# Attention and a routed expert layer on one core: side columns copied once per chunk, the last batch's routing moved by one slot, the first z chunk loaded in halves

## The chip, the cores and the metric

The kernel runs on one core of a Trainium2 chip. The metric is the device time of one execution in microseconds; the number that is compared is the median of several runs. One further execution is recorded by the hardware profiler, and all rows below come from that one.

## The reference

Eight batches of 2496 tokens, 256 wide. The first part is an attention without a softmax, gated by `u`; its result is the input of a layer of eight experts, of which each token uses one.

```python
scores = (1 / S) * z @ z.T            # per batch, z is 2496 x 64
x = u * (relu(scores) ** 2 @ v)       # 19968 rows of 256
logits = x @ w_gate + bias[modality]  # 8 experts
e = argmax(logits); gate = softmax(logits)[e]
out[row] = gate * (relu(x[row] @ w1[e]) @ w2[e])   # w1: 256 x 1024, w2: 1024 x 256
```

Everything is float32. The kernel gets the accuracy out of faster matmuls by splitting each operand into a high part and a low rest (`zm`, `vh`/`vl`, `ah`/`al`, `xh`/`xl`, `hh`/`hl`), and by multiplying high with high, high with low and low with high.

## The kernel before

**Phase 1** walks over the batches, in each over 5 chunks of up to 512 query columns, and in each chunk over ten steps of two blocks of 128 keys. A step is: scores on TensorE (L294), relu on ScalarE (L300), the square (L314), its split into `ah` (L338, ScalarE or VectorE) and `al` (L347, VectorE), and the product with `v` on TensorE (L363). At a chunk's end the sum is read out, transposed back to rows (L448) and multiplied by `u` (`take_rows`), so that `x` holds 4 blocks of 128 tokens ("columns", 20 in a batch). Each column then gets its eight logits on VectorE (L470, eight instructions of 256 elements), later the routing (`route_logits` to `route_gates`), which yields for each token a place in the list of its expert, and a scatter: VectorE copies the token's gate and number, two values, behind the 256 of its row (L581), and GpSimd writes the column's 128 rows to their places in DRAM with an indirect DMA (L583).

**Phase 2** walks over tiles of 512 rows of one expert (`run_tile`). A tile has slots f = 0 to 7 and two more. In slot f TensorE multiplies with a block of `w1` (`up`, L1048, the first matmul with `xh`, the second with `xl`), ScalarE takes the relu (`hh`, L1052), VectorE makes the rest (`hl`, L1053), and two slots later TensorE multiplies with `w2` (`down`, L1061 with `hh`, L1062 with `hl`). `finish` casts the row numbers (`ids`, L1072), scales the result on ScalarE and VectorE (L1077, L1079: four instructions `y`), and GpSimd scatters it to the output. The next tile's rows are transposed on VectorE (`xt`, L890) in slot 6 (slot 4 in the tile before tile -2), copied on ScalarE (`xh`, L897), and subtracted on VectorE (`xl`, L902).

Four tiles, t = -4 to -1, run before all tokens are routed. Into their 32 slots (slot 0 is tile -4, f = 0; slot 8 is tile -3, f = 0) a table of `put(slot, piece)` calls places what is left of the last batch: logits, four pieces of routing, the scatters of its last twelve columns, the plan of the remaining tiles (eight pieces, one-partition arithmetic on VectorE, L626 to L716), and the loads of the first planned weights. The engines run their instructions in the order in which the program issues them (`manual_schedule`), so the table sets the order on VectorE by hand. An instruction that comes late on VectorE makes every later `hl`, `xl` and `y` late.

At the **program's start** the SyncE queue issues the loads of `z` and `v` (L226, L157) in turn; TensorE runs matmuls on zeros (`warm`, L923) until `zm` is there: ScalarE makes its high part (L231), VectorE its low part (L236).

Of the kernel before, what the change touches and what calls it, by code (L numbers as in the profile page):

```python
# [9 lines left out]
F32 = mybir.dt.float32  # L10
# [3 lines left out]
ALU = mybir.AluOpType  # L14
AX = mybir.AxisListType
P = 128
T = 512
# [4 lines left out]
def ins_of(x):  # L22
    return getattr(x, "ins", x)
# [3 lines left out]
def tile_attention_moe(ctx: ExitStack, tc: tile.TileContext, u, v, zt, mid, wg, mb, w1, w2, out):  # L27
# [11 lines left out]
    nc = tc.nc  # L39
    B, S, D = u.shape  # L40
# [5 lines left out]
    J = T // P  # L46
# [5 lines left out]
    XW = D + 2  # L52
# [37 lines left out]
    def bank_tile(shape, name):  # L90
        return bank["pool"].tile(shape, F32, tag=bank["tag"], name=name)
# [4 lines left out]
    few = 128  # L96
# [27 lines left out]
    n = NCOL - J  # L124
# [97 lines left out]
    Z, V, zraw, vraw, U = {}, {}, {}, {}, {}  # L222

    def load_z(b, c):
        zr = raw.tile([P, T], F32, tag="zr", bufs=3, name="zr")
        nc.sync.dma_start(out=zr, in_=zt[b, :, c * T:(c + 1) * T])  # L226
        zraw[b, c] = zr

    def prep_z_high(b, c):
        zm = turned.tile([P, 2, T], F32R, tag="zm", bufs=NCH + 1, name="zm")  # L230
        nc.scalar.copy(out=zm[:, 0, :], in_=zraw[b, c])  # L231
        Z[b, c] = zm

    def prep_z_low(b, c):
        zm = Z[b, c]
        nc.vector.tensor_tensor(out=zm[:, 1, :], in0=zraw.pop((b, c)), in1=zm[:, 0, :].bitcast(F32), op=ALU.subtract)  # L236

    def load_v(b, c):
        vr = raw.tile([P, J, D], F32, tag="vr", bufs=3, name="vr")
# [223 lines left out]
    def logits(b, c, n):  # L463

        if c == 0 and n == 0:
            LG[b] = rows.tile([P, NCOL, E], F32, tag="lg", bufs=2, name="lg")
        x = X[b, c]
        for k in range(n * LG_STEP, (n + 1) * LG_STEP):
            j, e = k // E, k % E
            nc.vector.scalar_tensor_tensor(  # L470
                out=spare[:, k % 2, :],
                in0=x[:, j, 0:D],
                scalar=1.0,
                in1=wgb[:, e, :],
                op0=ALU.mult,
                op1=ALU.mult,
                accum_out=LG[b][:, c * J + j, e:e + 1],
            )
# [4 lines left out]
    RT = {}  # L483
# [92 lines left out]
    def scatter(b, k):  # L576

        c, j = k // J, k % J
        x = X[b, c]
        n = 64 if k == NCOL - 1 else P  # L580
        nc.vector.tensor_copy(out=x[:, j, D:XW], in_=RT[b]["side"][:, k, :])  # L581
        i = ins_of(
            nc.gpsimd.indirect_dma_start(  # L583
                out=xs,
                out_offset=bass.IndirectOffsetOnAxis(ap=RT[b]["sloti"][:n, k:k + 1], axis=0),
                in_=x[:n, j, :],
                in_offset=None,
                bounds_check=E * CAP - 1,
                oob_is_err=False,
            )  # L590
        )
        tc.declare_no_dep(i, group="xs", reason="each token has a row of its own")
        tc.add_to_no_dep_group("xs", i)
        scatters.append(i)
        if j == J - 1:
            X.pop((b, c))
# [149 lines left out]
    for b in range(B):  # L746
        g0 = b * per
        if b:
            for c in range(NCH):
                gz = g0 - 13 + 2 * c if c else g0 - 24  # L750
                gv = g0 - NI + 2 * c if c else g0 - 20
                at(gz - 3, load_z, b, c)
                at(gv - 3, load_v, b, c)
                queue(gz, g0 + 2 * c - 8, act(0.6, prep_z_high, b, c), dve(0.7, prep_z_low, b, c))
                queue(gv, g0 + 2 * c - 2, act(1.05, prep_v_high, b, c), dve(1.25, prep_v_low, b, c))
        for c in range(NCH):
            g = g0 + c * NI
            at(g + 5, load_u, b, c)
            at(g + NI - 1, evacuate_low, b, c, 0)
            at(g + NI - 1, evacuate_low, b, c, 1)  # L760
            if b < B - 1 or c < NCH - 1:
                for h in reversed(range(KD)):
                    queue(g + NI, g, dve(0.7, evacuate_high, b, c, h))
                at(g + NI, make_rows, b, c)
                for r in range(2):
                    queue(g + NI + 1, g + NI + 2, dve(0.7, take_rows, b, c, r))
                for n in range(LGN):
                    hurry = b == B - 2 and c == NCH - 1 or b == B - 1 and c == 1
                    queue(g + NI + 2, g + NI + ((7 if b < B - 1 else 5) + n // 3 if hurry else 8 + n // 2), dve(0.35 * LG_STEP, logits, b, c, n))

    def routing(b):

        pause = none(lambda: None)
        cols = WHOLE if b < B - 1 else SOON
        pieces = [dve(2.0, route_logits, b, cols), dve(1.9, route_places, b, cols), pause, none(route_count, b, cols)]
        pieces += [dve(2.6, lambda b: (route_slots(b, cols), route_gates(b, cols)), b)]
        hurry = J if b < B - 1 else 0
        pieces += [dve(0.2, lambda k=k: (scatter(b, k), scatter(b, k + 1))) for k in range(0, hurry, 2)]
        for k in range(hurry, cols.stop):
            pieces += [dve(0.1, scatter, b, k)] + [pause] * (b != B - 2)  # L780
        return pieces

    for e in range(E):
        for n in range(2):
            k = 2 * e + n
# [11 lines left out]
    for c in range(2, NCH):  # L797
        queue(max(1, 2 * c - 4), max(1, 2 * c - 4), act(0.6, prep_z_high, 0, c), dve(0.7, prep_z_low, 0, c))
        queue(2 * c - 2, 2 * c - 2, act(1.05, prep_v_high, 0, c), dve(1.25, prep_v_low, 0, c))
# [116 lines left out]
    for c in range(3):  # L916
        load_z(0, c)
        load_v(0, c)
    with tc.manual_schedule(engines={ET.PE, ET.Activation, ET.DVE, ET.Pool}):
        warm = [bank_tile([P, T], "warm") for _ in halves]  # L920
        for n in 4 * [few] + 6 * [T]:
            for x, h in zip(warm, halves):
                nc.tensor.matmul(out=x[:, 0:n], lhsT=zeros[h, 0:P], rhs=zeros[h, 0:n], start=True, stop=True)  # L923
        prep_z_high(0, 0)
        prep_z_low(0, 0)
        prep_v_first()
        scores(0)
# [4 lines left out]
        prep_z_low(0, 1)  # L932
        scores(1, True)
        load_z(0, 3)
        load_v(0, 3)
        square(1)
# [30 lines left out]
        for g in range(G):  # L967
            waiting += [(end, g, p) for end, p in due.pop(g, ())]
            b, c, i = steps[g]
# [217 lines left out]
    def put(slot, *pieces):  # L1187
        n, f = slots[slot]
        between[n][f] += pieces
# [1 line left out]
    put(0, lambda: part_weights_low(-1, KD))  # L1191
    put(3, lambda: part_weights_low(-1, KD + 1))
    for n, args in enumerate(left_over):
        put((1, 1, 11)[min(n, 2)], lambda args=args: logits(*args))
    for slot, n in zip((2, 3, 4, 4, 4, 5, 5, 5, 6, 7, 9, 9, 9, 10, 10, 10), range(LGN)):
        put(slot, lambda n=n: logits(B - 1, NCH - 1, n))
    for slot, pieces in ((12, (route_logits, route_exp)), (13, (route_places,)), (15, (route_count,)), (16, (route_slots, route_gates))):
        put(slot, *(lambda p=p: p(B - 1, LATE) for p in pieces))
    for n, k in enumerate(range(LATE.start, NCOL)):
        put(16 + n * 3 // 4, lambda k=k: scatter(B - 1, k))  # L1200
    planning = plan()
    for slot in (17, 18, 19, 20, 20, 21, 21, 22):
        put(slot, lambda: next(planning, None))
    put(22, lambda: fetch_weights(0))
    put(27, lambda: prefetch(-1), lambda: fetch_weights(1))
# [70 lines left out]
```

## Time and profile before

| | us |
|---|---|
| median of 3 runs | 2238.99 (2238.19 to 2239.13) |
| the profiled execution | 2237.93 |
| its span | 2236.1 |
| TensorE busy | 2213.1 (99%) |
| VectorE busy | 1805.5 (81%) |
| ScalarE busy | 1574.0 (70%) |
| GpSimd busy | 364.4 (16%) |
| mean granted clock | 0.996 of full speed |

The span is the time between the first and the last instruction of the profile; the profiled execution's own time is 1.83 us longer. The engines work side by side, so a busy share alone says little of a change in one place. The queries below look at the waits of TensorE and at the places that the table of slots touches. In the rows PE is TensorE, PEld its weight loads, DVE VectorE, ACT ScalarE, POOL GpSimd; `out<-in` names the buffers; a bracket at the end of a timeline row is the engine's idle time just before and what ended it.

### The profile page before, as it was taken

Reading aid. Unit: us, or ns where it says so; the run is one execution under the profiler, and the core shown is the slowest. Engines: PE = TensorE matmul, PEld = TensorE weight load, DVE = VectorE, ACT = ScalarE, POOL = GpSimd, SP = SyncE. Lnnn points to the kernel's source line nnn. Section 1 sums busy time; section 2 is a strip of 40 time slices with the busy share of each in tenths; the row PEclk is TensorE's granted clock in tenths of the full one; section 3 lists DMA queues with packets and bytes.
Section 4 is the critical chain, followed back from the end, with each engine's and each line's share of the span. In section 5 each row is a group of like instructions: output and inputs, shape, how many; then the busy total and the mean of one; then the engine's idle time right before and its main releaser. Section 6 shows DMA issues by size and latency. Waiting matters only on the chain.

```text
span 2236.1 us, 44437 instructions
## 1 busy us (share of the span) xinstructions
PE 2213.1 (99%) x16850; PEld 1867.1 (83%) x16850; DVE 1805.5 (81%) x4555; ACT 1574.0 (70%) x1919; POOL 364.4 (16%) x350
## 2 busy tenths in 40 slices
PE   9999999999999999999999999999999999999996
PEld 7888888888888888888888888788888888888885
DVE  7889989989989989989989998666666666666664
ACT  8888888888888888888888873455555555555553
POOL 0000220220220220220220422221212121111111
PEclk9999999999999999999999999999999999999998
DMA  6223223222112112112111122654545454545440
GB/s 195 102 71 106 78 92 113 74 77 76 34 58 75 34 57 75 36 58 73 39 47 39 51 89 62 180 167 119 164 122 162 123 161 124 159 124 160 127 150 23
DMA packets 199602, 216.64 MB, mean 97 GB/s; under 512 B 118448, under 2 KB 166064, under 8 KB 194512
## 3 DMA queue, kind: packets, MB, share of 16 engines
q1 hardware_dynamic: 184288, 172.49, 26.3%
q0 software_dynamic: 15088, 41.21, 5.0%
q8 instruction: 134, 2.20, 0.4%
q14 instruction: 92, 0.75, 0.1%
HBM read 168.23 MB, written 62.19 MB: 103 GB/s over the span
## 4 chain that ended last, share of the span: by engine, by line
PE 59%; issue 26%; DMA 9%; POOL 3%; DVE 1%; ACT 0%; POOLq 0%
PE acc L363 46%; PE s L294 12%; DMA out_dram<-y,ids 9%; POOL out_dram L1081 3%; PE po L448 1%; POOL xs L583 0%; POOLq L1081 0%; PE warm L923 0%; DVE hl L1053 0%; ACT r L298 0%; ACT vh L245 0%; ACT r L300 0%; ACT r L314 0%; ACT zm L231 0%; PE pc L547 0%
## 5 line engine op out<-in xcount | busy, mean ns | idle before, releaser
L300 ACT ACTIVATE r<-s 128x1024 f32<-128x1024 f32 (+1 forms) x395 | 397.4, 1006 | 180.9 <-PE s L294 176.2
L347 DVE TENSOR_TENSOR al<-r,ah 128x1024 fp32r<-128x1024 f32 (+1 forms) x359 | 429.6, 1197 | 78.1 <-ACT ah L338 61.6
L470 DVE SCALAR_TENSOR_TENSOR spare<-x,wgb 128x256 f32<-128x256 f32 x1280 | 462.2, 419 | 0.9
L1052 ACT ACTIVATE hh<-ph 128x512 fp32r<-128x512 f32 x312 | 186.3, 597 | 384.1 <-PE ph L1048 384.1
L1061 PE MATMUL po<-w,hh 128*128 128x512 f32 x1248 | 447.4, 394 | 0.0
L363 PE MATMUL acc<-ah,vh 64*128 64x512 f32 (+1 forms) x3120 | 434.4, 382 | 0.8 <-DVE ah L321 0.8
L1048 PE MATMUL ph<-xh,w 128*128 128x512 f32 x1248 | 427.4, 393 | 0.3 <-DVE x L418 0.3
L363 PE MATMUL acc<-al,vh 64*128 64x512 f32 (+1 forms) x3120 | 426.5, 381 | 0.0
L363 PE MATMUL acc<-ah,vl 64*128 64x512 f32 (+1 forms) x3120 | 424.8, 382 | 0.0
L314 ACT ACTIVATE r<-r 128x1024 f32<-128x1024 f32 (+2 forms) x401 | 416.9, 1040 | 3.3
L1053 DVE SCALAR_TENSOR_TENSOR hl<-ph,hh 128x512 fp32r<-128x512 f32 x312 | 215.4, 690 | 213.9 <-ACT hh L1052 213.6
L583 POOL DMA_INDIRECT xs<-x,sloti x160 | 204.5, 1278 | 1000.0 <-DVE x L581 953.8
L1062 PE MATMUL po<-w,hl 128*128 128x256 f32 x1248 | 349.4, 280 | 2.6 <-DVE hl L1053 2.6
L363 PEld LDWEIGHTS acc<-ah,vh 64*128 64x128 f32 x3120 | 299.6, 184 | 55.2 <-DVE ah L321 1.3
L363 PEld LDWEIGHTS acc<-al,vh 64*128 64x128 f32 x3120 | 299.8, 184 | 54.8
L363 PEld LDWEIGHTS acc<-ah,vl 64*128 64x128 f32 x3120 | 292.5, 184 | 54.5
L294 PE MATMUL s<-zm 64*128 64x512 f32 (+1 forms) x2400 | 336.8, 386 | 0.7 <-ACT r L300 0.7
L338 ACT CAST ah<-r 128x1024 fp32r<-128x1024 f32 (+1 forms) x282 | 287.1, 1018 | 0.0
L1061 PEld LDWEIGHTS po<-w,hh 128*128 128x128 f32 x1248 | 235.0, 188 | 54.3
L1048 PEld LDWEIGHTS ph<-xh,w 128*128 128x128 f32 x1248 | 234.8, 188 | 54.4 <-DVE x L418 0.7
L1081 POOL DMA_INDIRECT out_dram<-y,ids x157 | 152.8, 973 | 706.8 <-DVE y L1079 678.7
L294 PEld LDWEIGHTS s<-zm 64*128 64x128 f32 x2400 | 221.8, 185 | 40.2 <-ACT r L300 1.4
(164 smaller groups left out, 1955.7 us busy)
## 6 DMA issues: line engine op xcount, KB each, us to landing
w<-w1s SPq DMA_DIRECT2D x37, 1024.0 KB
w<-w2s SPq DMA_DIRECT2D x37, 1024.0 KB
xg<-xs SPq DMA_DIRECT2D x156, 128.0 KB
vr<-in_v_dram SPq DMA_DIRECT2D x32, 512.0 KB
ut<-in_u_dram SPq DMA_DIRECT2D x32, 512.0 KB
zr<-in_zt_dram SPq DMA_DIRECT2D x40, 256.0 KB
w1s<-in_moe_w_dram SPq DMA_DIRECT2D x16, 512.0 KB
w2s<-in_moe_w_dram SPq DMA_DIRECT2D x8, 1024.0 KB
```

What stands on the lines that cost most here:

```text
L294: nc.tensor.matmul(out=s[t][:, :w], lhsT=lhs, rhs=mv[halves[t], ql, :w], start=n == 0, stop=n == 2)
L300: nc.scalar.activation(out=r[:, :, :w], in_=both[:, :, :w], func=AF.Relu, scale=INV)
L314: nc.scalar.square(out=a[:, t, :w], in_=r[:, t, :w])
L338: copy(out=ah[:, :, :w], in_=st_a[g][:, :, :w])
L347: nc.vector.tensor_tensor(out=al[:, :, :w], in0=a[:, :, :w], in1=ah[:, :, :w].bitcast(F32), op=ALU.subtract)
L363: nc.tensor.matmul(out=acc[b, c][r][dh][:, :w], lhsT=V[b, k // J][y][halves[r], k % J, dh * P:(dh + 1) * P], rhs=x[halves[r], k % 2, :w], ...
L470: nc.vector.scalar_tensor_tensor(out=spare[:, k % 2, :], in0=x[:, j, 0:D], scalar=1.0, in1=wgb[:, e, :], op0=ALU.mult, op1=ALU.mult, accum ...
L1048: nc.tensor.matmul(out=ph, lhsT=lhs, rhs=rhs[:, k, :], start=n == 0, stop=n == 3 * KD - 1)
L1053: nc.vector.scalar_tensor_tensor(out=hl, in0=ph, scalar=0.0, in1=hh.bitcast(F32), op0=ALU.max, op1=ALU.subtract)
L1061: nc.tensor.matmul(out=po[j], lhsT=hh[:, s], rhs=both, start=f == 0, stop=False, skip_group_check=True)
L1062: nc.tensor.matmul(out=po[j][:, 0:D], lhsT=hl[:, s], rhs=w[:, 0, :], start=False, stop=f == KF - 1, skip_group_check=True)
L1081: nc.gpsimd.indirect_dma_start(out=out, out_offset=bass.IndirectOffsetOnAxis(ap=ids[:, j:j + 1], axis=0), in_=y, in_offset=None, bounds_ch ...
```

## The change

Three edits. The copy of gate and token number is issued once per chunk, for its four columns together, before the chunk's first scatter, and no longer in front of each scatter. In the table of slots the last batch's routing, scatters and plan come one slot earlier, and the last two of the four left-over units of logits of the chunk before come in slot 7 and no longer in slot 11. The first chunk of `z` is loaded, copied and subtracted in two halves of 256 columns, and one pair of the `warm` matmuls is left out.

```diff
--- before.py
+++ after.py
@@ -223,17 +223,24 @@
 
     def load_z(b, c):
         zr = raw.tile([P, T], F32, tag="zr", bufs=3, name="zr")
-        nc.sync.dma_start(out=zr, in_=zt[b, :, c * T:(c + 1) * T])
+
+        n = 1 if b or c else 2
+        for i in range(n):
+            s = slice(i * T // n, (i + 1) * T // n)
+            nc.sync.dma_start(out=zr[:, s], in_=zt[b, :, c * T + s.start:c * T + s.stop])
         zraw[b, c] = zr
 
     def prep_z_high(b, c):
         zm = turned.tile([P, 2, T], F32R, tag="zm", bufs=NCH + 1, name="zm")
-        nc.scalar.copy(out=zm[:, 0, :], in_=zraw[b, c])
+        for s in (slice(0, T),) if b or c else (slice(0, T // 2), slice(T // 2, T)):
+            nc.scalar.copy(out=zm[:, 0, s], in_=zraw[b, c][:, s])
         Z[b, c] = zm
 
     def prep_z_low(b, c):
         zm = Z[b, c]
-        nc.vector.tensor_tensor(out=zm[:, 1, :], in0=zraw.pop((b, c)), in1=zm[:, 0, :].bitcast(F32), op=ALU.subtract)
+        zr = zraw.pop((b, c))
+        for s in (slice(0, T),) if b or c else (slice(0, T // 2), slice(T // 2, T)):
+            nc.vector.tensor_tensor(out=zm[:, 1, s], in0=zr[:, s], in1=zm[:, 0, s].bitcast(F32), op=ALU.subtract)
 
     def load_v(b, c):
         vr = raw.tile([P, J, D], F32, tag="vr", bufs=3, name="vr")
@@ -578,7 +585,8 @@
         c, j = k // J, k % J
         x = X[b, c]
         n = 64 if k == NCOL - 1 else P
-        nc.vector.tensor_copy(out=x[:, j, D:XW], in_=RT[b]["side"][:, k, :])
+        if not j:
+            nc.vector.tensor_copy(out=x[:, :, D:XW], in_=RT[b]["side"][:, k:k + J, :])
         i = ins_of(
             nc.gpsimd.indirect_dma_start(
                 out=xs,
@@ -918,7 +926,7 @@
         load_v(0, c)
     with tc.manual_schedule(engines={ET.PE, ET.Activation, ET.DVE, ET.Pool}):
         warm = [bank_tile([P, T], "warm") for _ in halves]
-        for n in 4 * [few] + 6 * [T]:
+        for n in 4 * [few] + 5 * [T]:
             for x, h in zip(warm, halves):
                 nc.tensor.matmul(out=x[:, 0:n], lhsT=zeros[h, 0:P], rhs=zeros[h, 0:n], start=True, stop=True)
         prep_z_high(0, 0)
@@ -1191,15 +1199,15 @@
     put(0, lambda: part_weights_low(-1, KD))
     put(3, lambda: part_weights_low(-1, KD + 1))
     for n, args in enumerate(left_over):
-        put((1, 1, 11)[min(n, 2)], lambda args=args: logits(*args))
+        put((1, 1, 7)[min(n, 2)], lambda args=args: logits(*args))
     for slot, n in zip((2, 3, 4, 4, 4, 5, 5, 5, 6, 7, 9, 9, 9, 10, 10, 10), range(LGN)):
         put(slot, lambda n=n: logits(B - 1, NCH - 1, n))
-    for slot, pieces in ((12, (route_logits, route_exp)), (13, (route_places,)), (15, (route_count,)), (16, (route_slots, route_gates))):
+    for slot, pieces in ((11, (route_logits, route_exp)), (12, (route_places,)), (14, (route_count,)), (15, (route_slots, route_gates))):
         put(slot, *(lambda p=p: p(B - 1, LATE) for p in pieces))
     for n, k in enumerate(range(LATE.start, NCOL)):
-        put(16 + n * 3 // 4, lambda k=k: scatter(B - 1, k))
+        put(15 + n * 3 // 4, lambda k=k: scatter(B - 1, k))
     planning = plan()
-    for slot in (17, 18, 19, 20, 20, 21, 21, 22):
+    for slot in (16, 17, 18, 19, 19, 20, 21, 21):
         put(slot, lambda: next(planning, None))
     put(22, lambda: fetch_weights(0))
     put(27, lambda: prefetch(-1), lambda: fetch_weights(1))
```

In the changed file the lines from L231 on stand 7 or 8 lines further down: L581 is L589, L890 is L898, L1053 is L1061.

The order on VectorE at the end of tile -4 (slot 7), before and then after. The rows L470 (L477 after) are the logits, two of the logits instructions and then six.

```order
L890 STREAM_TRANSPOSE xt<-xg 128x1024
L1053 SCALAR_TENSOR_TENSOR hl<-ph,hh 128x512
L470 SCALAR_TENSOR_TENSOR spare,lg<-x,wgb 128x256 x2
L902 TENSOR_TENSOR xl<-xt,xh 128x1024
L1072 CAST ids<-gate 128x4
L1079 SCALAR_TENSOR_TENSOR y<-po,gate,part_19439 128x256
```

```order
L898 STREAM_TRANSPOSE xt<-xg 128x1024
L1061 SCALAR_TENSOR_TENSOR hl<-ph,hh 128x512
L477 SCALAR_TENSOR_TENSOR spare,lg<-x,wgb 128x256 x6
L910 TENSOR_TENSOR xl<-xt,xh 128x1024
L1080 CAST ids<-gate 128x4
L1087 SCALAR_TENSOR_TENSOR y<-po,gate,part_19333 128x256
```

Four more logits instructions stand between the tile's last `hl` and the next tile's `xl`.

VectorE at the end of tile -3 and the start of tile -2 (slots 15 and 16), before and after. `at` to `side` are `route_slots` and `route_gates`; `y` is the output of tile -3; `hl` is the first of tile -2.

```order
L1072 CAST ids<-gate 128x4
L1079 SCALAR_TENSOR_TENSOR y<-po,gate,part_19690 128x256
L1079 SCALAR_TENSOR_TENSOR y<-po,gate,part_19701 128x256
L1079 SCALAR_TENSOR_TENSOR y<-po,gate,part_19712 128x256
L1079 SCALAR_TENSOR_TENSOR y<-po,gate,part_19723 128x256
L1053 SCALAR_TENSOR_TENSOR hl<-ph,hh 128x512
L553 TENSOR_TENSOR at<-pc,base 128x8
L555 TENSOR_TENSOR base<-pc,base 128x8
L556 TENSOR_TENSOR run<-run,at 128x160
L557 TENSOR_TENSOR run<-run,hot 128x160
L559 TENSOR_REDUCE slot<-run 128x20
L561 CAST sloti<-slot 128x20
```

```order
L568 CAST sloti<-slot 128x20
L574 TENSOR_REDUCE sm<-ex 128x12
L575 TENSOR_SCALAR sm<-sm 128x12
L578 RECIPROCAL side<-sm 128x12
L579 TENSOR_SCALAR side<-tok 128x12
L589 COPY x<-side 128x4x2
L1080 CAST ids<-gate 128x4
L1087 SCALAR_TENSOR_TENSOR y<-po,gate,part_19602 128x256
L1087 SCALAR_TENSOR_TENSOR y<-po,gate,part_19613 128x256
L1087 SCALAR_TENSOR_TENSOR y<-po,gate,part_19624 128x256
L1087 SCALAR_TENSOR_TENSOR y<-po,gate,part_19635 128x256
L1061 SCALAR_TENSOR_TENSOR hl<-ph,hh 128x512
```

Routing stood behind tile -2's first `hl`; now it ends ahead of tile -3's `ids` and `y`, followed by one copy for the whole chunk (`128x4x2`).

VectorE at the end of tile -2 (slots 21 to 23), before and after. `p_i`, `meta` and `p_off` belong to the last two pieces of the plan.

```order
L1053 SCALAR_TENSOR_TENSOR hl<-ph,hh 128x512
L581 COPY x<-side 128x2 x2
L712 SCALAR_TENSOR_TENSOR p_i<-p_i,p_off 1x42
L713 TENSOR_TENSOR p_i<-p_i,p_last 1x42
L714 SCALAR_TENSOR_TENSOR p_i<-p_ex,p_i 1x42
L716 CAST meta<-p_i 1x42
L716 CAST meta<-p_ex 1x42
L890 STREAM_TRANSPOSE xt<-xg 128x1024
L1053 SCALAR_TENSOR_TENSOR hl<-ph,hh 128x512
```

```order
L718 TENSOR_REDUCE p_off<-p_ge 1x42
L720 SCALAR_TENSOR_TENSOR p_i<-p_i,p_off 1x42
L721 TENSOR_TENSOR p_i<-p_i,p_last 1x42
L722 SCALAR_TENSOR_TENSOR p_i<-p_ex,p_i 1x42
L724 CAST meta<-p_i 1x42
L724 CAST meta<-p_ex 1x42
L1061 SCALAR_TENSOR_TENSOR hl<-ph,hh 128x512
L898 STREAM_TRANSPOSE xt<-xg 128x1024
L1061 SCALAR_TENSOR_TENSOR hl<-ph,hh 128x512
```

The two copies behind the tile's seventh `hl` are gone, and the plan's end stands ahead of that `hl`, so that between the tile's last two `hl` only the transpose `xt` is left.

## Rows read from the trace of the kernel before

**Rows 1.** which engine is busy; section 1 of the page: busy us, share, instructions.

```profile
PE 2213.1 (99%) x16850; PEld 1867.1 (83%) x16850; DVE 1805.5 (81%) x4555; ACT 1574.0 (70%) x1919; POOL 364.4 (16%) x350
```

**Rows 2.** TensorE's waits over the run: us in total, times, longest.

```profile
PE po L1062 <- DVE hl L1053: 2.6, 2, 2.1
...
PE s L294 <- ACT r L300: 0.7, 1, 0.7
```

**Rows 3.** windows: length, busy (count) by engine, PEclk, DMA share, GB/s.

```profile
700.00:1300.00 600.00, 600.00 (x5588) 504.70 (x5586) 549.81 (x1715) 511.28 (x563) 106.83 (x86) 1.00 0.16 51
...
1407.85:1411.26 3.41, 3.41 (x13) 2.92 (x12) 2.55 (x5) 1.35 (x3) 1.92 (x3) 0.50 0.89 305
```

**Rows 4.** timeline of TensorE, end of tile -2: start, us, tile, [idle before].

```profile
1403.74 0.40 PE L1061 MATMUL po<-w,hh 128*128 128x512 f32 x1
1404.61 0.39 PE L1062 MATMUL po<-w,hl 128*128 128x256 f32 x1 [0.48 <-DVE hl L1053]
1404.84 0.39 PE L1061 MATMUL po<-w,hh 128*128 128x512 f32 x1
1407.35 0.39 PE L1062 MATMUL po<-w,hl 128*128 128x256 f32 x1 [2.12 <-DVE hl L1053]
...
1411.18 0.44 PE L1048 MATMUL ph<-xh,w 128*128 128x512 f32 x1
```

**Rows 5.** timeline of TensorE, end of tile -4 and the next tile's start.

```profile
1359.01 0.39 PE L1061 MATMUL po<-w,hh 128*128 128x512 f32 x1
...
1361.80 0.39 PE L1048 MATMUL ph<-xh,w 128*128 128x512 f32 x1
1362.03 0.40 PE L1048 MATMUL ph<-xl,w 128*128 128x512 f32 x1
```

**Rows 6.** timeline of VectorE through tile -2.

```profile
1386.50 0.69 DVE L1053 SCALAR_TENSOR_TENSOR hl<-ph,hh 128x512 fp32r<-128x512 f32 x1 [1.03 <-ACT hh L1052]
1387.11 0.15 DVE L553 TENSOR_TENSOR at<-pc,base 128x8 f32<-128x8 f32 x1
...
1389.43 0.24 DVE L581 COPY x<-side 128x2 f32<-128x2 f32 x2
...
1403.47 0.49 DVE L710 TENSOR_REDUCE p_off<-p_ge 1x42 f32<-1x336 f32 x1
1403.89 0.67 DVE L1053 SCALAR_TENSOR_TENSOR hl<-ph,hh 128x512 fp32r<-128x512 f32 x1
...
1406.64 0.65 DVE L1053 SCALAR_TENSOR_TENSOR hl<-ph,hh 128x512 fp32r<-128x512 f32 x1
```

**Rows 7.** timeline of VectorE at the end of tile -4.

```profile
1359.05 0.41 DVE L470 SCALAR_TENSOR_TENSOR spare<-x,wgb 128x256 f32<-128x256 f32 x1
...
1359.74 1.22 DVE L902 TENSOR_TENSOR xl<-xt,xh 128x1024 fp32r<-128x1024 f32 x1
```

**Rows 8.** VectorE by line, 1378.0 to 1386.6: busy us, mean ns | idle before.

```profile
L1079 DVE SCALAR_TENSOR_TENSOR y<-po,gate,part 128x256 f32<-128x256 f32 x4 | 1.9, 484 | 2.0 <-ACT part L1077 2.0
```

**Rows 9.** timeline of ScalarE at the start of the program.

```profile
3.71 0.62 ACT L231 CAST zm<-zr 128x512 fp32r<-128x512 f32 x1 [1.67 <-DMA zr<-in_zt_dram]
4.97 0.62 ACT L256 CAST vh<-vr 128x512 fp32r<-128x512 f32 x1 [0.65 <-DMA vr<-in_v_dram]
5.89 1.08 ACT L298 ACTIVATE r<-s 128x512 f32<-128x512 f32 x2 [0.29 <-PE s L294]
```

**Rows 10.** VectorE by line, 100 to 1300.

```profile
L581 DVE COPY x<-side 128x2 f32<-128x2 f32 x140 | 21.4, 162 | 0.0
```

**Rows 11.** timeline of VectorE and GpSimd: subtracts without and beside scatters.

```profile
1044.62 1.23 DVE L347 TENSOR_TENSOR al<-r,ah 128x1024 fp32r<-128x1024 f32 x1 [0.57 <-ACT ah L338]
...
1073.34 1.23 POOL L583 DMA_INDIRECT xs<-x,sloti  x1 [61.80 <-DVE x L581]
...
1075.90 1.22 DVE L347 TENSOR_TENSOR al<-r,ah 128x1024 fp32r<-128x1024 f32 x1
...
1076.22 1.76 POOL L583 DMA_INDIRECT xs<-x,sloti  x1 [0.30 <-issue]
```

## Prediction

> **What bounds the kernel now.** I read the busy shares first: TensorE is busy 99% of the span [rows 1], so a change gains only where TensorE waits or runs at a lower clock, and loses only where it makes TensorE wait. Its waits come next. They add up to little: the largest by far is the matmul with `hl` in the early tiles, 2.6 us in two pieces, and there is one of 0.7 us early in phase 1 [rows 2]. The windows show the rest of the run as TensorE's: in 600 us of phase 1 it has no idle time, beside a VectorE busy 549.81 us; but for 3.41 us after 1407.85 its granted clock is 0.50, which of the two levels is 1.2 GHz and not 2.4 [rows 3]. The timeline puts the two waits and that stretch at one place, the end of tile -2 (slots 22 and 23): idle 0.48 us, 2.12 us, and then the slow clock until 1411.18, when the next tile's first `up` starts [rows 4]. What this place costs I read against the end of tile -4, where nothing waits: from the last-but-seven `hh` matmul to the next tile's first `up`, the same eight pairs, 1361.80 − 1359.01 = 2.79 us [rows 5]. Here it took 1411.18 − 1403.74 = 7.44. **The loss is 4.65 us**, 2.6 of it idle, the rest refill and slow clock.
>
> Who is late there is VectorE. From tile -2's first `hl` at 1386.50 to the end of its last (1406.64 + 0.65 = 1407.29) it runs through without a pause, so each instruction taken out of this stretch brings the last `hl` forward by its own length [rows 6].
>
> **The table of slots and the copies.** In that stretch the routing piece `route_slots` and `route_gates` goes: it ran from 1387.11 to the copy at 1389.43, 2.32 us [rows 6]. The table put the twelve scatters into slots 16, 16, 17, 18, 19, 19, 20, 21, 22, 22, 23, 24, each behind its slot's `hl`, so ten copies ran before the `hl` of slot 23; now there is one for each of three chunks, in slots 15, 18 and 21, so two stay in the stretch. A pair of them is listed with 0.24 us and a single one takes 0.162 us [rows 6, 10], so one more costs about 0.07: eight of them 0.54 us. Against it, the plan's reduction at 1403.47 takes 0.49; now its reader follows at once, where before the `hl` at 1403.89 stood between them [rows 6]: 1403.47 + 0.49 + 0.03 (the usual gap) − 1403.89 = 0.10 us of waiting for the result. The last `hl` ends at 1407.29 − 2.32 − 0.54 + 0.10 = 1404.53. The matmul that reads it started 0.06 after its end [rows 4, 6], so 1404.59.
>
> When does TensorE want it? The `hh` matmul at 1403.74 takes 0.23 to its successor, a pair takes 2.79 / 8 = 0.349 [rows 5], so undisturbed, with 0.12 for the first `hl` matmul and 0.23 for the next `hh`, the second `hl` matmul stands at 1403.74 + 0.349 + 0.23 = 1404.32. **A wait of 0.27 us is left**. After a wait the `hl` matmul took 0.23 to its successor where it else takes 0.12 [rows 4]: 0.11 more. Together 0.38. Does the clock fall again? It fell behind two waits of 0.48 and 2.12 us close together [rows 3, 4]; what a single wait of 0.3 us does no row here shows. I take no fall, since the idle time left is a tenth of that; the other case is a rival below.
>
> Where the routing goes, slot 15, it stands ahead of tile -3's `ids` and four `y`. VectorE idles 2.0 us in front of these `y`, waiting for ScalarE [rows 8], and 1.03 us in front of the next `hl` [rows 6]; 2.32 + 0.07 us goes into these 3.0. That costs nothing as long as the `y` end before 1386.50; beyond that, each 0.1 us goes into the stretch above again. Queued behind the `y` are only GpSimd's output scatters, for which no engine waits. The first routing pieces and the scatters also come a slot earlier; GpSimd's queue then takes the tile's output scatters in another order with those of `xs`, both without a reader near. The weight load for the first planned tile, behind the plan on the SyncE queue, starts some 3 us earlier.
>
> **The logits in slot 7.** They move from a place inside tile -3 to the end of tile -4, behind its last `hl` and ahead of `xl`. Two ran there, from 1359.05 to 1359.74, 0.345 each [rows 7]; four more take 1.38 us. `xl` started at 1359.74 and took 1.22, ending at 1360.96; now it ends at 1362.34. The next tile's second `up` matmul, which reads it, ran at 1362.03 [rows 5]. **A new wait of 1362.34 + 0.05 − 1362.03 = 0.36 us**, with 0.10 of refill 0.46. Behind `xl` stand tile -4's `ids` and `y`, later by the same 1.38 us; the next reader of VectorE there is the new tile's first `hl`, and its reader on TensorE stands two slots further. Nothing waits for it.
>
> **Copies in phase 1.** Of the 140 copies in 100 to 1300 us, 21.4 us in all [rows 10], three in four go, some 7 us of VectorE's time. TensorE never waits for VectorE there [rows 3], so this is worth nothing to the end. GpSimd, which waited for each copy, will instead run four scatters in a row, and all four columns' scatters wait for one copy that is issued no later than the first was.
>
> **The start.** ScalarE waits 1.67 us for the first `z`, then 0.65 us for `v` [rows 9], on which everything up to the first product hangs. Halves may land the first 256 columns earlier, but the transfers share the same engines, and one more issue puts `v` about 0.4 us later in its queue. ScalarE's first relu waits 0.29 us for TensorE's scores [rows 9]; that is the most an earlier `z` can give. A later `v` delays the copy ahead of that relu by up to 0.4 and takes back the same 0.29 first, so it costs 0.1 at most; an unlucky DMA 0.3. Later, TensorE's 0.7 us wait for ScalarE's relu [rows 2] passes the gain or loss of ScalarE on. From −0.3 to +0.3, I take −0.1, nearer to the middle than to an end because both halves hang on the same transfers. The `warm` pair left out ran while TensorE had nothing else.
>
> **The sum**, against the profiled execution's 2237.93: −4.65 + 0.38 + 0.46 − 0.10 = −3.91, so 2234.02. The median of before lies 1.06 above that execution, and I keep the distance: **2235.1 us**, 0.17% faster.
>
> **The rivals.**
>
> *Nothing waits* (0.25). Both small waits above are differences of 0.3 us between sums of several terms. If VectorE comes 0.3 us sooner (copies dearer than 0.07, as a single copy's 0.162 [rows 10] would have it: 8 × 0.162 = 1.30 for 0.54) and the start gives its 0.3, the whole 4.65 and 0.3 are gained, less the 0.46 or nothing: 2238.99 − 4.95 + 0.0 to 0.46 = 2234.0 to 2234.5.
>
> *The clock falls again* (0.09). If the last `hl` is late by more than 0.27, because slot 15's `y` push the stretch back or the plan's steps wait for one another more than once, 3.41 us at half clock [rows 3] cost 1.7 us again: 2235.1 + 1.7 = 2236.8, and with a wait of 1.2 us 2237.7. Against it: the sum takes away 2.86 us of work for 2.4 us of waits.
>
> *GpSimd's rows of four slow VectorE: slower* (0.06). The 140 copies belong to 35 chunks [rows 10], whose scatters were spread by the copies and now can run back to back; at 1.23 to 1.76 us each [rows 11] four take some 5 us. VectorE has 50 us of air in 600 [rows 3], 9%. If VectorE's work, most of it split subtracts (`al`, 1.22 us), takes over 9% longer beside the scatters, it becomes the bound there, and each 10% beyond that costs 0.5 us a chunk: 35 × 0.5 − 3.9 = +13.6, 2252.6. Against it: `al` took 1.23 us with GpSimd idle for 60 us, and 1.22 beside a scatter that followed the one before without a wait [rows 11]. The Trainium skill (GPSIMD Engine Reference, section "Specifications") says that GpSimd's way into SBUF is shared with VectorE, with contention when a VectorE instruction has two SBUF inputs, which `al` has; by it this rival would be the likely case. The two rows above do not show it for these scatters, and the measurement decides.
>
> *The change does less than it says.* Were only the copies to count, and the moved routing to come back in as idle time before the `y`, the first wait would shrink by 0.54 us alone and the clock still fall: 2238.99 − 0.54 + 0.46 = 2238.9. It has 0.02 of the second rival's 0.09.
>
> **How the numbers follow.** The forecast has 0.60; its own range, with both small waits and the start together 1.1 us better or worse, is 2234.0 to 2236.2. The time of the second rival's far end (2238) and of the first's near end with the median's own scatter of some 0.5 us (2233.4) bound the range: 2233.4 to 2238.0. What a measurement of this kernel can tell from no change is about 0.2%, 4.5 us, so faster means under 2234.5. That takes in the first rival and a fifth of the forecast's cases: 0.25 + 0.12 = 0.37. Slower is the third rival: 0.06. The rest, 0.57, is the same.
>
> **What would show it.** Right: TensorE's waits list 0.2 to 0.4 us for `hl` and as much for `xl` (L1056 reading `xl` after 1362), no window with a clock of 0.50 after tile -2, VectorE idle before `y` of tile -3 near 0.6 in all; `al` at 1.22 in rows of four scatters. Wrong: a second wait at tile -2's end over 0.5 us, or the clock falling once more; a new wait in tiles -3 or -1; TensorE waiting for `al` in phase 1.

## The result and the profile after

The changed kernel is **slower**: median 2243.69 us (2242.25 to 2245.94, 14 runs) beside 2238.46 (2237.02 to 2239.93, 14 runs) of the kernel before on the same chip; ratio 1.0022, 95% interval 1.0014 to 1.0031. That is +5.2 us where 3.9 us of gain was forecast, outside the range, on the wrong side.

The profiled execution took 2245.94 us with a span of 2244.2, so it lies 2.3 us above the median; its losses are a little larger than the typical ones. Following one instruction through both traces shows where the time goes (the start of the same relu on ScalarE, or of the last matmul, before and after):

| instruction | before | after | lag |
|---|---|---|---|
| first relu of phase 1 | 5.89 | 7.87 | 1.98 |
| a relu at the end of the start | 13.97 | 17.58 | 3.61 |
| a relu of batch 1 | 258.61 | 263.70 | 5.09 |
| first relu of tile -2 | 1385.87 | 1391.66 | 5.79 |
| first relu of tile -1 | 1412.82 | 1420.16 | 7.34 |
| last matmul | 2218.23 | 2225.57 | 7.34 |

So the loss has three places: the start, something near 250 us, and tile -2, where a gain was forecast. First TensorE's waits in the changed kernel, beside [rows 2]:

```profile
PE acc L370 <- DVE ah L328: 2.8, 1, 2.8
PE s L301 <- ACT r L307: 1.5, 2, 1.2
PE po L1069 <- issue: 1.1, 1, 1.1
PE po L1070 <- DVE hl L1061: 1.1, 1, 1.1
PE po L1070 <- issue: 1.0, 1, 1.0
...
PE ph L1056 <- DVE xl L910: 0.2, 1, 0.2
```

The 2.6 us for `hl` of [rows 2] have become 1.1, the forecast wait for `xl` is there with 0.2, and waits that the profile puts down to nothing ("issue") are new. The wait for `ah` at the start has grown from 0.8 to 2.8 us; its line in the kernel before:

```profile
PE acc L363 <- DVE ah L321: 0.8, 1, 0.8
```

**The start**, ScalarE's timeline, beside [rows 9]:

```profile
3.06 0.71 ACT L236 CAST zm<-zr 128x256 fp32r<-128x256 f32 x2 [1.02 <-DMA zr<-in_zt_dram]
7.34 0.62 ACT L263 CAST vh<-vr 128x512 fp32r<-128x512 f32 x1 [3.57 <-DMA vr<-in_v_dram]
7.87 1.08 ACT L305 ACTIVATE r<-s 128x512 f32<-128x512 f32 x2
```

The halves of `z` are there 0.65 us sooner, but `v` lands at 7.34 and not at 4.97. TensorE then has nothing to do for 2.8 us, and its clock falls. The windows (length, busy time and count by engine, granted clock, DMA share, GB/s) of the changed kernel, beside [rows 3]:

```profile
1407.00:1410.00 3.00, 2.98 (x8) 2.15 (x7) 1.84 (x5) 1.08 (x2) 0.00 (x0) 0.50 0.00 0
10.80:13.80 3.00, 3.00 (x16) 2.33 (x14) 2.90 (x6) 2.97 (x5) 0.00 (x0) 0.50 1.04 427
3.00:4.00 1.00, 1.00 (x8) 0.73 (x6) 0.50 (x2) 0.71 (x2) 0.00 (x0) 1.00 0.56 152
```

From 3 to 4 us the transfers move 152 GB/s at a DMA share of 0.56; before it was 379 GB/s at 0.98 in the same stretch:

```profile
3.00:4.00 1.00, 1.00 (x8) 0.80 (x6) 0.00 (x0) 0.29 (x1) 0.00 (x0) 1.00 0.98 379
```

Both stretches of 3 us in which the clock is 0.50 come behind TensorE's waits.

**Tile -2**, ScalarE, slots 18 to 21, and TensorE's last matmul for the first late relu:

```profile
1394.46 0.60 ACT L1060 ACTIVATE hh<-ph 128x512 fp32r<-128x512 f32 x1 [0.81 <-PE ph L1056]
1401.67 0.60 ACT L1060 ACTIVATE hh<-ph 128x512 fp32r<-128x512 f32 x1 [6.61 <-remote]
1407.46 1.08 ACT L1060 ACTIVATE hh<-ph 128x512 fp32r<-128x512 f32 x2 [5.20 <-remote]
```

```profile
1396.81 0.40 PE L1056 MATMUL ph<-xh,w 128*128 128x512 f32 x1
```

The input of the relu at 1401.67 was done at 1397.21 (1396.81 + 0.40). ScalarE had been idle since 1395.06 and still began 4.46 us late; the next relu, 5.20 us late. "remote" is the profile's word for a releaser that it does not find. The trace itself shows which side was late. ScalarE waits here for a semaphore, a counter by which TensorE tells it that a matmul has ended, and the trace holds the time of each raise. For the relu at 1394.46, which was in time, the raise is recorded at 1394.43, 0.01 us after the matmul's end. For the relu at 1401.67 it is recorded at 1401.64, 4.43 us after the matmul's end, and for the next relu at 1407.44. Each time ScalarE starts within 0.03 us of the raise: it answered at once, and the signal of TensorE came late.

The same at 250 us (TensorE's scores end at 251.94; the relu starts at 254.80, 2.86 us later):

```profile
251.00 0.94 PE L301 MATMUL s<-zm 64*128 64x512 f32 x6
```

```profile
250.11 1.08 ACT L321 ACTIVATE r<-r 128x1024 f32<-128x1024 f32 x1
254.80 1.02 ACT L307 ACTIVATE r<-s 128x1024 f32<-128x1024 f32 x1 [3.61 <-PE acc L370]
```

At both places GpSimd is in the middle of a run of scatters with nothing between them (0.30 us apart, "issue"), eight from 244.84 to 256.4 and twelve from 1390.15 to 1405.8:

```profile
249.55 0.98 POOL L591 DMA_INDIRECT xs<-x,sloti  x1 [0.30 <-issue]
250.84 1.51 POOL L591 DMA_INDIRECT xs<-x,sloti  x1 [0.30 <-issue]
252.65 1.07 POOL L591 DMA_INDIRECT xs<-x,sloti  x1 [0.30 <-issue]
...
1399.11 0.98 POOL L591 DMA_INDIRECT xs<-x,sloti  x1 [0.30 <-issue]
1400.40 0.98 POOL L591 DMA_INDIRECT xs<-x,sloti  x1 [0.30 <-issue]
1401.68 0.97 POOL L591 DMA_INDIRECT xs<-x,sloti  x1 [0.30 <-issue]
```

In the kernel before the runs in phase 1 were of five at most.

In what follows a **late start** is a relu of ScalarE that begins over 0.25 us after both its input matmul and ScalarE's last instruction have ended, counted over all 717 relus of a trace. The first trace of before has none; the changed kernel's has thirteen, all of them during or right behind scatters of `x`: 2.86 us at 252 us, 4.46 and 5.20 in tile -2, 1.5 once in each of six batches (mostly made good later), and four under 0.7. Their size does not follow the length of the run: the six of 1.5 us stand behind runs of four, and the later runs of eight in phase 1 have 0.3 us or none.

### The profile page after: what moved, and what is told of

The parts are those of the page before. It is cut to its first block, busy times and chain, and to the rows that moved or that the text cites. A ratio compares the mean times of both kernels' runs of the same rounds, so it can differ in the third digit from the quotient of the medians.

```text
span 2244.2 us, 44216 instructions
## 1 busy us (share of the span) xinstructions
PE 2216.7 (99%) x16848; PEld 1868.0 (83%) x16848; DVE 1797.9 (80%) x4436; ACT 1574.5 (70%) x1920; POOL 348.9 (16%) x350
## 4 chain that ended last, share of the span: by engine, by line
PE 61%; issue 24%; DMA 9%; POOL 3%; another core or an unknown queue 1%; DVE 0%; ACT 0%; POOLq 0%; SPq 0%
PE acc L370 46%; PE s L301 12%; DMA out_dram<-y,ids 9%; POOL out_dram L1089 3%; PE ph L1056 1%; PE po L455 1%; PE po L1069 1%; PE po L1070 0%; DMA vr<-in_v_dram 0%; POOLq L1089 0%; POOL xs L591 0%; DVE spare L477 0%; DVE hl L1061 0%; ACT r L307 0%
## 5 line engine op out<-in xcount | busy, mean ns | idle before, releaser
L477 DVE SCALAR_TENSOR_TENSOR spare<-x,wgb 128x256 f32<-128x256 f32 x1280 | 462.5, 421 | 0.9
L1061 DVE SCALAR_TENSOR_TENSOR hl<-ph,hh 128x512 fp32r<-128x512 f32 x312 | 215.7, 691 | 219.2 <-ACT hh L1060 188.0
L591 POOL DMA_INDIRECT xs<-x,sloti x160 | 188.4, 1178 | 1024.5 <-DVE x L589 930.3
```

The source lines that it names most:

```text
L477: nc.vector.scalar_tensor_tensor(out=spare[:, k % 2, :], in0=x[:, j, 0:D], scalar=1.0, in1=wgb[:, e, :], op0=ALU.mult, op1=ALU.mult, accum ...
L1061: nc.vector.scalar_tensor_tensor(out=hl, in0=ph, scalar=0.0, in1=hh.bitcast(F32), op0=ALU.max, op1=ALU.subtract)
```

## Experiments

The theories: **A**, the loss is the start. **B**, it is the runs of scatters behind one copy. After the first four runs B became **C**: a run of scatters without a break makes TensorE's signals to ScalarE late, and so ScalarE's starts, whichever edit lengthens the run. Against it **D**: late starts come at any time and have nothing to do with scatters.

All medians, beside the kernel before on the same chip in the same job:

| run | edits | median | before | difference | ratio, 95% |
|---|---|---|---|---|---|
| e1 | halved z alone | 2239.81 | 2238.27 | +1.5 | 0.9996 to 1.0015 |
| e2 | copies alone | 2239.60 | 2238.27 | +1.3 | 0.9994 to 1.0012 |
| e3 | slots alone | 2240.28 | 2238.27 | +2.0 | 1.0001 to 1.0019 |
| e4 | copies and slots | 2242.38 | 2238.27 | +4.1 | 1.0011 to 1.0029 |
| e13 | before + short rest | 2238.39 | 2238.24 | +0.2 | 0.9990 to 1.0008 |
| e14 | e3 + short rest | 2235.40 | 2238.24 | -2.8 | 0.9978 to 0.9996 |
| e11 | e4 + short rest | 2234.80 | 2238.53 | **-3.7** | 0.9975 to 0.9993 |
| e17 | e4 + shortest rest | 2235.18 | 2238.48 | -3.3 | 0.9977 to 0.9995 |
| e12 | e11, logits in slot 11 | 2235.20 | 2238.53 | -3.3 | 0.9976 to 0.9994 |
| e15 | all edits + short rest | 2235.46 | 2238.24 | **-2.8** | 0.9979 to 0.9997 |
| e16 | e15, v between the halves | 2236.29 | 2238.24 | -2.0 | 0.9983 to 1.0001 |
| e7 to e10 | with a long rest | 2255 to 2261 | 2238.69 | +16 to +23 | |

### One edit at a time

e1 takes from the change the three hunks on z and `warm`, e2 the copy per chunk alone, e3 the table alone (two of its lines are shown), e4 the last two together.

```diff
@@ e2 @@
-        nc.vector.tensor_copy(out=x[:, j, D:XW], in_=RT[b]["side"][:, k, :])
+        if not j:
+            nc.vector.tensor_copy(out=x[:, :, D:XW], in_=RT[b]["side"][:, k:k + J, :])
@@ e3 @@
-        put(16 + n * 3 // 4, lambda k=k: scatter(B - 1, k))
+        put(15 + n * 3 // 4, lambda k=k: scatter(B - 1, k))
...
-    for slot in (17, 18, 19, 20, 20, 21, 21, 22):
+    for slot in (16, 17, 18, 19, 19, 20, 21, 21):
```

> The kernel before with the halved first z and one warm pair less, nothing else. Theory A (the loss is the start): in the changed kernel's profile v lands at 7.34 us and not at 4.97, TensorE then waits 2.8 us for ah and runs 3 us at half clock; by 1300 us it is 5.3 us behind. So this kernel should be slower by 3.5 to 5.3 us. Theory B (the loss is in the runs of four scatters, behind one copy a chunk): this kernel stays within 1 us of before. My prediction's term was -0.1.

> The kernel before with one copy per chunk, nothing else. Theory A: no change in phase 1, and the wait at the end of tile -2 shrinks by about 0.5 us: -0.5 to 0. Theory B: the late answers seen at 250 us and in tile -2 of the changed kernel (ScalarE idle 3.6, 6.6 and 5.2 us with its input done) come from the runs of scatters: slower by 2 to 5 us, and such idle times in the profile.

> The kernel before with the new table of slots, nothing else. Both theories: the stall at the end of tile -2 is mostly gone, with the copies still there (0.54 us more work before the last hl than in the changed kernel) and the new wait for xl: -4.65 + 0.9 + 0.46 = -3.3, if the clock stays up; -1.6 if it falls again.

> The changed kernel without the halved z and with the warm pair back. Theory A: my prediction without its start term, -3.8 us (2234.7 on the earlier median). Theory B: slower than before by 0 to 3 us, with ScalarE's idle times in tile -2 again.

None of the three edits gains. e1 and e2 alone are not clear of no change, but the three differences add up (1.5 + 1.3 + 2.0 = 4.8, where the whole change lost 5.2). The start is a part, not the whole: A alone is wrong. Most telling is e3: both theories expected -3.3, and it lost 2.0, though its profile lists only 0.8 us of waiting for `hl`. Its ScalarE in tile -2:

```profile
1396.48 0.60 ACT L1052 ACTIVATE hh<-ph 128x512 fp32r<-128x512 f32 x1 [6.57 <-remote]
1400.87 1.09 ACT L1052 ACTIVATE hh<-ph 128x512 fp32r<-128x512 f32 x2 [3.79 <-remote]
```

Late by 4.41 and 3.79 us, without the single copy per chunk. What e3 shares with the changed kernel here is GpSimd: two scatters of `x`, the four output scatters of tile -3, which wait for the later `y`, and four more of `x` follow one another, ten in a row from 1385.0 to 1397.5. In e2 the late starts are those of phase 1 (3.58 us at 248, 1.5 once in most batches) and two in tile -2 (0.94 and 1.83).

### Both kernels recorded again

e5 and e6 are the kernel before and the changed kernel, unchanged, one execution each (2239.12 and 2244.82 us).

> The kernel before, unchanged, profiled a second time beside the next run. Theory C (TensorE's signals to ScalarE come late while GpSimd issues scatters without a pause): the profile has ScalarE's idle times at 250 us and in tile -2 neither in this run nor in the first. Theory D (such late signals happen in any kernel's profiled execution from time to time): they are here too, somewhere, with idle times of 2 us and more while the input is done.

> The changed kernel, unchanged, profiled a second time. Theory C: ScalarE idles at the same two places as in the first profile, for 2 to 6 us. Theory D: at other places or not at all. Theory A: v lands at 7 us again and TensorE's half clock near 11 us is there again.

The changed kernel has its late starts at the same places again (2.87 at 251 us, 1.5 once in each of six batches, 3.06 and 6.59 in tile -2), and `v` lands at 6.36. The kernel before, which showed none the first time, now has eight: 0.65 to 0.71 us behind the run of five scatters of each of six batches, 0.98 and 0.47 in tile -2. This is the first of them; the input was done at 247.74 + 0.94 = 248.68, the relu began at 249.39:

```profile
249.39 1.03 ACT L300 ACTIVATE r<-s 128x1024 f32<-128x1024 f32 x1 [1.45 <-PE s L294]
```

Neither expectation for e5 came true as written: C had none here, D had 2 us and more. But all eight stand at runs of scatters, as do the five of 0.3 to 0.7 us in e1's trace, whose runs in phase 1 are of five at most as well. That speaks for C and against D; what decides is to break the runs.

### A rest between scatters

If C holds, breaking the run must bring the forecast back. The rest is a tile of its own that nothing reads:

```diff
+    rest = small.tile([P, 60], F32, name="rest")
...
         scatters.append(i)
+        for _ in range(10):
+            nc.gpsimd.memset(rest, 0.0)
```

> e2 (one copy per chunk, nothing else) with a rest of GpSimd, ten small memsets of about 0.1 us, behind each scatter of x, so that no two such scatters follow each other within 1 us. Theory C (a run of scatters without a pause makes TensorE's signals to ScalarE late): ScalarE's late starts at 250, 310, 476 us and in tile -2 are gone, 1 to 2 us less than e2's median: -0.5 to +0.3 against before. Theory D (late starts have nothing to do with the scatters' spacing): like e2, +1.3.

> e4 (copies per chunk and the new slots, the start as before) with the same rest behind each scatter. Theory C: tile -2 loses neither to the late hl nor to late signals; my prediction's sum without the start: -4.65 + 0.38 + 0.46 = -3.8, so 2234.5 beside 2238.3. Theory D: like e4, +4.

> e8 with the two left-over units of logits back in slot 11. Theory C: e8 less the wait for xl, 0.2 us by the changed kernel's profile (0.46 in my prediction): 2234.2. Against it: the routing in slot 11 then comes 1.4 us later on VectorE, which may make an hl of tile -3 late.

> The changed kernel with the rest behind each scatter. Theory C: e8 plus the start's loss, which e1 measured as +1.5 (0.0 to 3.3): 2236.0, some 7 us less than the changed kernel. Theory D: like the changed kernel, +5.

All four lost 16 to 23 us: ten memsets make it 3.6 us from one scatter of `x` to the next, too much. The last batch's last scatter starts at 1436.89 in e8, the next tile's rows, which are gathered from what the scatters write, come late, and VectorE's queue waits for them; a memset of `x` stands behind the rests as well. TensorE's waits in e8:

```profile
PE po L1066 <- DVE hl L1057: 12.8, 2, 12.6
PE po L431 <- POOL x L413: 3.6, 1, 3.6
```

But in the traces of e7 and e8 there is not one late start, and between the first relu of tile -2 and that of tile -1 e8 gains 4.3 us on e5, what the prediction said of that place. So a shorter rest, `range(3)`:

> e8 with three memsets of rest and not ten: a scatter every 2.2 us instead of 3.6, so that the twelve scatters of the last batch end by 1416 us as in the kernel before, and the memset of x at 1340 us is not kept waiting. Theory C: late starts of ScalarE under 0.5 us everywhere, the end of tile -2 gains 4.2 us as it did in e8, nothing is late behind it: -3.8, 2234.6. If a rest this short does not separate the scatters enough: 2238 to 2242.

> e11 with the two left-over units of logits back in slot 11: e11 less the 0.2 to 0.4 us of the wait for xl, or more where an hl of tile -3 comes late.

e11 reaches 2234.8, -3.7, **faster than both kernels**. No late start. GpSimd in tile -2:

```profile
1397.05 0.97 POOL L585 DMA_INDIRECT xs<-x,sloti  x1 [0.61 <-issue]
1398.02 0.58 POOL L598 MEMSET rest<- 128x60 f32 x3
1399.26 0.97 POOL L585 DMA_INDIRECT xs<-x,sloti  x1 [0.67 <-DVE p_ge L703]
```

ScalarE at the place that was late, now 2.17 us idle because TensorE works on its next input, as it did in the kernel before:

```profile
1397.73 0.60 ACT L1056 ACTIVATE hh<-ph 128x512 fp32r<-128x512 f32 x1 [2.17 <-PE ph L1052]
1400.49 0.60 ACT L1056 ACTIVATE hh<-ph 128x512 fp32r<-128x512 f32 x1 [2.17 <-PE ph L1052]
```

And the window in which the changed kernel had a clock of 0.50:

```profile
1407.00:1410.00 3.00, 3.00 (x16) 2.47 (x15) 1.91 (x6) 1.46 (x3) 1.64 (x6) 1.00 0.99 350
```

e12 is no faster than e11 (0.4 us apart, within what the runs can tell): the wait for `xl` is gone from its trace, and one of 0.2 us for `hl` has come. With the long rest the same edit came out 0.7 us faster (e9 beside e8), so no gain or loss is shown.

### Control, and each edit with the rest

> The kernel before with the short rest (three memsets) behind each scatter, nothing else: the control. Theory C: the kernel before loses little to late signals (0.4 us by its second profile), so -0.5 to 0. If the rest itself were the gain of e11, this would show -3 to -4.

> e3 (the new slots, copies per column, start as before) with the short rest. Theory C: e3's +2.0 was the run of ten scatters in tile -2, with ScalarE starting 4.4 and 3.8 us late; with rests -3.3, 2235. Otherwise +2 as e3.

> The whole changed kernel with the short rest: e11 plus the price of the halved z alone. By e1 +1.5 (0 to 3.3): 2236.3. In the profile v lands after 5.5 us; where TensorE then waits over 1.5 us for ah its clock is 0.50 for 3 us near 11 us.

> e15 with the first v's load issued between the two halves of z instead of behind both. If the place in the queue makes v late (0.46 us of issue): v lands by 5.1 us again, and the start costs 0 to 0.5 us against e11. If the transfers of 256 columns are slow themselves (3 to 4 us in the changed kernel: 152 GB/s where before had 379): v or the second half lands late still, and it costs 1 us or more.

The control decides it: the rest gives the kernel before nothing (+0.2), so it is no gain of its own, but it turns the slots from +2.0 to -2.8 (e3, e14), the slots and copies from +4.1 to -3.7 (e4, e11), and the **whole change from +5.2 to -2.8** (e15). Its 2235.46 stands beside the forecast 2235.1, its -2.8 beside -3.9, but it is not the kernel that was forecast, and the start is in it with a loss for a gain. None of e13 to e16 has a late start.

The halved z with everything else quiet costs 0.9 us by the differences of e15 and e11, 0.5 by e10 and e8 in one job (2256.29 and 2255.83). Neither is clear of nothing by itself; with e1's 1.5 they agree in sign. In e15's trace, an execution 1.8 us above its median, `v` is late and the clock is down again, as in e1 and e6 (0.66 from 9 to 14 us in both); in e10, where TensorE waits 0.3 us for `ah`, it stays at 1.00:

```profile
6.40 0.62 ACT L264 CAST vh<-vr 128x512 fp32r<-128x512 f32 x1 [2.60 <-DMA vr<-in_v_dram]
```

```profile
3.00:4.00 1.00, 1.00 (x8) 0.70 (x6) 0.58 (x2) 0.79 (x2) 0.00 (x0) 1.00 0.61 143
9.00:14.00 5.00, 5.00 (x34) 4.05 (x36) 4.89 (x8) 4.17 (x8) 0.00 (x0) 0.73 1.00 384
```

e16 issues `v` between the halves:

```diff
             nc.sync.dma_start(out=zr[:, s], in_=zt[b, :, c * T + s.start:c * T + s.stop])
+            if n > 1 and not i:
+                load_v(0, 0)
...
-        load_v(0, c)
+        if c:
+            load_v(0, c)
```

It does not help (0.8 us slower than e15): now the second half is late.

```profile
2.95 0.40 ACT L239 CAST zm<-zr 128x256 fp32r<-128x256 f32 x1 [0.91 <-DMA zr<-in_zt_dram]
5.55 0.40 ACT L239 CAST zm<-zr 128x256 fp32r<-128x256 f32 x1 [2.19 <-DMA zr<-in_zt_dram]
5.86 0.61 ACT L266 CAST vh<-vr 128x512 fp32r<-128x512 f32 x1
```

From 3 to 4 us e16 moves 340 GB/s, so it is not the halves as such that are slow; with both halves first the transfers are idle for part of that time (a share of 0.56 and 0.61), and with `v` between them the second half is there at 5.55, where the whole load of before was at 3.71. By the medians one whole load of z, then `v`, is the best of the three orders, though their intervals overlap.

### How long a rest

> e11 with one memset of rest instead of three, about 1.8 us from scatter to scatter. If a short break is enough: -3.7 as e11, ScalarE nowhere late by over 0.25 us. If the rate must fall further: late starts of 1 to 3 us in tile -2 again and a time between e11 and e4, 2236 to 2241.

One memset is enough: -3.3, no late start. GpSimd in tile -2:

```profile
1392.91 0.97 POOL L585 DMA_INDIRECT xs<-x,sloti  x1 [0.30 <-issue]
1393.88 0.17 POOL L598 MEMSET rest<- 128x60 f32 x1
1394.21 0.97 POOL L585 DMA_INDIRECT xs<-x,sloti  x1 [0.16 <-issue]
1395.17 0.18 POOL L598 MEMSET rest<- 128x60 f32 x1
1395.51 1.02 POOL L585 DMA_INDIRECT xs<-x,sloti  x1 [0.16 <-issue]
```

My expectation of 1.8 us from scatter to scatter was wrong: they follow each other after 1.30 us, where they did after 1.28 in the changed kernel (medians of phase 1: 1.48 and 1.47). So it is not the rate of scatters that makes ScalarE late, but that no other GpSimd instruction stands between those of `x`. The four output scatters of each tile still follow one another 0.30 us apart here, without a late start; in the seven traces that have late starts one such run in phase 2's later tiles has one behind it (e4, 1.19 us at 1821).

## Why the prediction was wrong

- **The step that failed** stands under "Copies in phase 1" and in the table's paragraph: "GpSimd, which waited for each copy, will instead run four scatters in a row", worth nothing, and "GpSimd's queue then takes the tile's output scatters in another order with those of `xs`, both without a reader near". I costed GpSimd's queue by who reads its results. Its price was another: while scatters follow one another without a break, TensorE's signals come late and with them ScalarE's starts. It is 8.0 us of the 9.1 between forecast and result (e15's -2.8 against the change's +5.2), shown by the rest and its control.
- **The slower rival** named the right place, the rows of scatters, with the wrong mechanism. VectorE's `al` was not slowed: its mean is 1198 ns over 324 instructions in the changed kernel from 100 to 1300 us (the line below), and 1198 in the kernel before. The Trainium skill (GPSIMD Engine Reference, section "Specifications") says that GpSimd contends with VectorE instructions of two SBUF inputs; here as before no trace shows it for these scatters.

```profile
L354 DVE TENSOR_TENSOR al<-r,ah 128x1024 fp32r<-128x1024 f32 (+1 forms) x324 | 388.1, 1198 | 70.4 <-ACT ah L345 52.9 <-ACT r L307 2.5 <-PE acc L370 0.6
```

- **The table of slots and the copies** were sized right. The end of tile -2 gained the forecast -4.65 + 0.38 once the starts were in time: e11 gains 4.4 us there on e5 (first relu of tile -2 to that of tile -1), and lists no wait for `hl` at all where 0.27 was forecast; e17 lists 0.5.
- **The logits in slot 7**: the new wait for `xl` is there, 0.2 us idle where 0.36 was forecast.
- **The start** was outside its bounds. I allowed ±0.3 and took -0.1; it cost 0.5 to 0.9 us (e10, e15) and 1.5 in e1. I bounded it by the waits for z and by 0.4 us of issue. What failed is "it costs 0.1 at most; an unlucky DMA 0.3": with both halves first `v` came at 5.76 to 7.34 us in five traces, at 4.83 to 5.56 in the thirteen with one load. From 3 to 4 us the transfers ran at 106 to 152 GB/s there and at 348 to 412 here; e10, at 106, has the earliest `v` of the five, so that microsecond alone does not set how late it comes. In the changed kernel TensorE waited 2.8 us behind it, and then its clock was at 0.50 for 3 us. The Trainium skill (DMA: Bandwidth & Descriptors, section "Bandwidth") gives 138 GB/s for a transfer of 64 KB and 341 for 1 MB, measured on transfers that GpSimd issued. The halves are 128 KB, issued by SyncE; the five traces agree with the direction, e16's 340 GB/s does not, so the order of the loads counts as well. I did not weigh that rule.
- **"I take no fall" of the clock** held where it was meant: in e11 and e17 the clock stays at 1.00 behind tile -2. In the changed kernel itself it fell to 0.50 there, as the second rival had it, but behind the late starts and not behind a late `y` or plan.

What stays open: why TensorE's signals come late. Of the 74 late starts in the seven traces that have any, 72 come within 0.03 us of a recorded raise of TensorE's semaphore, so it is the signal that is late there and not ScalarE. TensorE itself shows gaps of 1.0 and 1.1 us put down to "issue" in the same stretch, so it need not be that signal alone. The same seven traces lack 317 to 410 records of raises by TensorE, VectorE and ScalarE, out of some 6800; the first trace of the kernel before and the eleven with a rest lack hardly any. Whether lost records and late signals have one cause, and whether the recording takes part in it, no run here tells. And the first trace of the kernel before has no late start, the second eight small ones, so a run without a break does not always bring them.

## What to carry to other kernels

Before taking a wait out of GpSimd's queue, look at what its instructions then stand next to: indirect DMAs back to back cost other engines time here that no dependence shows, and one cheap instruction between them avoided it. An engine whose results nobody waits for is not free. Test an edit that looks worth nothing or less alone, too: the slots alone lost 2.0 us here and hid a gain of 2.8.

## What the hardware showed that was not expected

- Runs of 4 to 12 indirect scatters 0.30 us apart, with no other GpSimd instruction between them, made ScalarE begin up to 6.7 us after its input was done and it was free (e4), because TensorE's semaphore was raised that late; with one memset of 0.17 us between them and nearly the same spacing (1.30 us to 1.28), no start of 717 was over 0.25 us late (e17).
- The first load of `z` in two DMAs of 256 columns, both ahead of `v`, made `v` land later: at 5.76 to 7.34 us in five traces, against 4.83 to 5.56 in the thirteen with one load.
